# One DRAM read in place of five for the attention outputs of segments 0 to 2, with the features of a head dealt out in fives

## The chip, the core and the metric

The kernel runs on one core of a Trainium2 chip. The metric is device time in microseconds (us). The core has a matrix engine (PE), a vector engine (DVE), a scalar engine (ACT), a general one (POOL), and SyncE (SP), which here issues nearly all transfers. Each engine works through its own queue in the order in which it was written, and waits on semaphores for what other engines and transfers have to deliver. Matrix products go to PSUM, in eight banks; everything else is computed from SBUF.

## The reference

```python
# x: (2048, 640) bf16; H = 32 heads, Dh = 20; N = 4 segments of L = 512 tokens
q, k, v = heads of x @ wq, x @ wk, x @ wv
phi = lambda t: where(t > 0, t + 1, exp(t));  g = sigmoid(beta)
M = 0; z = 0                                     # a memory per head
for s in range(4):
    p = softmax(qs @ ks.T * Dh**-0.5 + causal mask)
    a_dot = p @ vs
    a_mem = (phi(qs) @ M) / (phi(qs) @ z + 1e-6)
    o[s] = g * a_mem + (1 - g) * a_dot
    M += phi(ks).T @ vs;  z += sum(phi(ks))
a = o @ wo
b = irfft2(rfft2(x) * (w_r + 1j * w_i))          # over tokens and features
t = sigmoid((x * gate_w).sum(-1))                # a gate per token
return t * a + (1 - t) * b
```

## The kernel before

There are two branches that share the engines: attention in four segments, and the two-dimensional spectral filter, done as matrix products with tables. Nothing decides an order at run time. The program lists its operations with their dependences, and a long tuple of numbers, `ORDER`, says in which order they go onto the five queues and, for operations that DVE or POOL could do, which of the two does it. A planner then places PSUM banks and semaphores along that order by rough costs (the `QUEUE` table has those of transfers); it moves nothing.

**Attention, segments 0 to 2.** Scores are computed for groups of four heads, exponentiated by ACT into `ex`, and masked by POOL (line 1299). The product with the values (`pv_flipped`) leaves outputs with features in rows, 32 rows a head (20 features, the denominator in row 20, padding), and 512 tokens in columns. ACT or DVE copies them to `ub`, and `st_u` stores two groups at a time in the DRAM scratch `u_scr` (3 segments of 1024 rows of 512 tokens). When a segment is done, `denominators` loads the denominators (`ld_den`, tile `dnc`), takes reciprocals (`dnr`), multiplies with the gate (`rc`) and stores the result in `r_scr` (`st_r`).

**The way back.** `finish_tile(s, 0)` loads the reciprocals (`ld_r`, tile `r`: each head's row in four partitions), and the outputs as `oU`: 128 partitions, four to a head, and five blocks `c` of 512 tokens, so that a partition has five of the head's 20 features. One load `ld_u` (line 1540) fills one block, for all 128 partitions. The `normal` step (line 1542, DVE or POOL) multiplies each block with `r`. For segments 1 and 2, `addmem` (line 1550) adds the memory's part: the memory was read in `mem_read`, divided by `mem_mul` (line 1172 for segments 1 and 2, 1175 for the last), stored in `o_scr`, and comes back by transposing loads as `mT`. The five blocks are then multiplied with the rows of `wo` that fit them (`ld_wo` loads these, one tile `wo` per block), in `finish_tile` (line 527 in the profile), which accumulates onto the gated spectral part and stores the result. Segment 3 goes another way, without `u_scr`.

**Where the blocks are written.** Each `oU` takes memory that something else used. For segment 0 it is that of the spectral branch's middle part (`after_mid`), for segment 1 the tile `phq`, for segment 2 the first values tile `va`.

**Around it.** While the way back runs, the spectral branch does its last part: 32 products of `Cp` with `big` into one PSUM bank each, which ACT or DVE copies to `eo`, or DVE combines with `eo` into `G` (line 1501). These and other single-bank products share four of the eight banks (`gen`); the scores have the other four. A gate per token goes through `omh`, `gT`, `g_scr`, `gbc` and `fbg`.

The way a block is dealt out before, in two lines of the code: row `4 * c + q` of a head goes to partition `q` of its four, block `c`; the same split stands in `ld_wo` and in `mem_mul`.

Of the kernel before, what the change touches and what calls it, by code (L numbers as in the profile page):

```python
# [12 lines left out]
P = 128  # L13
S = 2048
D = 640
H = 32
DH = 20
NSEG = 4
L = 512
KD = 321  # L20
VW = 22
# [424 lines left out]
def dap(ap, off, *dims):  # L446
    return bass.AP(tensor=ap.tensor, offset=ap.offset + off, ap=[list(q) for q in dims])
# [25 lines left out]
class Kern:  # L473
# [10 lines left out]
    def b(self, *key):  # L484
        v = self.bufs.get(key)
        if v is None:
            v = self.bufs[key] = Buf(str(key))
        return v
# [68 lines left out]
    def dma(self, dst, src, nbytes, r, w, prio, tr=False, name="", after=(), queue="sp"):  # L557
# [15 lines left out]
        "ld_hm": (600.0, 850.0, 16), "ld_r": (570.0, 700.0, 16), "ld_tt": (530.0, 1650.0, 16), "ld_u": (530.0, 600.0, 16),  # L573
# [86 lines left out]
        3616, 3446, 3618, 4034, 1577, 1610, 3156, 3176, 3620, 4016, 3622, 3158, 1634, 3154, 4102, 3606, 3624, 1636, 3626, 1638, 3178, 3628, 3448,  # L660
        3198, 3608, 3166, 1641, 1642, 3430, 3200, 1652, 3610, 3168, 1616, 1618, 3612, 4030, 1620, 1644, 3170, 1654, 1623, 1646, 4028, 3654, 1656,
        1648, 3160, 3184, 4042, 3584, 3656, 1658, 1650, 3162, 3670, 3250, 3658, 3587, 1688, 3146, 3660, 3672, 1690, 2940, 1692, 3164, 3187, 1624,
        1670, 1626, 4046, 1628, 4019, 1695, 3180, 2564, 1630, 3674, 1696, 1632, 1698, 3182, 1700, 3214, 3202, 1702, 1660, 3216, 1678, 3188, 1672,
        4036, 1680, 1674, 1662, 1704, 3462, 1664, 1682, 1676, 3588, 1666, 3206, 3218, 4038, 1742, 1684, 3204, 3208, 1750, 4020, 1744, 1668, 1746,
        3224, 1686, 3220, 1724, 1752, 1726, 4044, 1754, 1728, 1796, 3591, 3226, 1748, 3230, 3222, 1730, 3598, 1756, 3232, 3464, 1798, 3210, 1800,
        3600, 1732, 1758, 4080, 1734, 3228, 1736, 3602, 3238, 1803, 3470, 3212, 3604, 3630, 1738, 3240, 3706, 3234, 3632, 3638, 1740, 3708, 1706,
        3236, 3634, 1708, 3646, 3636, 1710, 4049, 4086, 3640, 3648, 3242, 1713, 3710, 4090, 3650, 3642, 1778, 4023, 3652, 1780, 3244, 3688, 3644,
        1714, 3690, 1716, 3246, 1782, 1804, 1718, 1806, 3692, 3694, 4024, 1808, 1720, 1760, 3714, 4082, 1784, 1810, 3662, 4089, 1722, 4094, 1850,
        3664, 1812, 3592, 1852, 1854, 3594, 1786, 3696, 3248, 1788, 1762, 1790, 4040, 1858, 1860, 4222, 1862, 4032, 1764, 1856, 4092, 3748, 1766,
        1792, 3678, 4206, 3750, 4208, 1864, 3666, 4210, 4098, 4212, 4214, 1794, 1768, 3676, 4510, 1770, 1866, 1772, 4216, 4026, 4050, 3596, 4064,  # L670
        4052, 4054, 4218, 3466, 3680, 1774, 3752, 1832, 4158, 3682, 1834, 3700, 1836, 1776, 4056, 4066, 3754, 4068, 3252, 4070, 4072, 4058, 4150,
        3668, 1840, 1842, 4074, 4154, 1838, 4084, 3756, 4076, 3698, 4146, 1844, 3758, 3716, 1814, 1846, 1816, 4142, 3702, 3718, 3720, 3684, 1848,
        4138, 3722, 3254, 3760, 4060, 4100, 3256, 4192, 4194, 3724, 3686, 4196, 3726, 4062, 3774, 4096, 1818, 4078, 3776, 1886, 3728, 3762, 4198,
        4200, 1820, 3468, 4202, 4104, 1888, 3778, 1822, 1824, 4224, 1826, 1890, 3766, 3786, 1828, 4354, 4226, 3764, 1893, 3768, 4228, 4230, 3780,
        1830, 4106, 4108, 4205, 4110, 3788, 4112, 4136, 4114, 4240, 3782, 4242, 4116, 4220, 4232, 3790, 4234, 4119, 3792, 3784, 3802, 3794, 3804,
        1894, 1896, 3704, 1898, 3806, 1900, 3808, 3770, 3796, 4244, 3772, 3810, 4236, 1902, 4246, 4248, 4250, 4238, 3812, 3798, 3852, 3814, 4120,
        3854, 4253, 3800, 4122, 4124, 1876, 4148, 4254, 3818, 3820, 4156, 1868, 3822, 4140, 4256, 1870, 1872, 4144, 3824, 1874, 4152, 3928, 3712,
        3826, 3732, 3828, 3930, 1878, 1880, 3734, 3736, 3830, 4160, 3856, 4320, 3738, 4357, 4176, 3932, 3740, 4126, 4178, 3742, 4128, 4130, 3744,
        4180, 4486, 3860, 4132, 4182, 3730, 3862, 1882, 3747, 4184, 4134, 4274, 4358, 4360, 4362, 3864, 4186, 4258, 4364, 4366, 4368, 4189, 3866,
        4418, 3920, 4370, 1884, 3858, 4490, 3922, 4276, 4322, 4260, 4372, 4262, 3868, 4374, 4452, 4376, 4378, 4380, 4264, 4278, 4382, 4280, 4492,  # L680
        4266, 3924, 4385, 3834, 4282, 3934, 3836, 4268, 4324, 4270, 4326, 3833, 4162, 4273, 4328, 4284, 4330, 4164, 4287, 4166, 3870, 4168, 4332,
        4170, 4288, 4334, 3816, 3842, 3838, 4336, 4402, 3844, 4404, 3872, 4406, 4172, 4408, 3936, 4388, 4175, 4338, 4340, 3874, 4390, 4342, 4190,
        4290, 3846, 4420, 4292, 4294, 4410, 3840, 4344, 4346, 4348, 3878, 3848, 4351, 4296, 3880, 4392, 4412, 4352, 3850, 4394, 4298, 4415, 3888,
        3876, 3890, 3892, 3894, 3882, 3884, 4304, 3896, 4396, 4300, 3898, 3886, 4398, 4306, 4302, 4308, 3938, 4454, 4400, 3904, 4488, 3940, 3906,
        4416, 3908, 3910, 3900, 3926, 4310, 4312, 3912, 4314, 4456, 3914, 4458, 4317, 4470, 4472, 3942, 3946, 3916, 4318, 4460, 3948, 4436, 3902,
        4474, 3944, 4462, 4464, 4438, 3950, 4466, 4440, 3952, 4442, 4469, 4476, 4444, 3958, 4478, 4422, 3964, 3954, 3974, 3960, 3966, 4480, 4424,
        4426, 3956, 4483, 4428, 4446, 4430, 4432, 4484, 3962, 3976, 3968, 3978, 4435, 4386, 3970, 3980, 4448, 4498, 3972, 3982, 4494, 3984, 3990,
        4450, 3992, 4496, 3986, 3994, 3996, 4500, 3989, 4548, 3998, 4526, 4512, 4000, 4620, 3919, 4514, 4002, 4528, 4634, 4516, 4622, 4004, 4636,
        4502, 4506, 4504, 4518, 4509, 4550, 4638, 4530, 4640, 4642, 4532, 4644, 4552, 4534, 4647, 4520, 4624, 4522, 4536, 4626, 4525, 4628, 4538,
        4562, 4564, 4566, 4568, 4546, 4540, 4630, 4570, 4554, 4633, 4542, 4544, 4598, 4556, 4600, 4572, 4654, 4648, 4602, 4604, 4575, 4558, 4650,  # L690
        4652, 4606, 4584, 4561, 4608, 4586, 4588, 4611, 4590, 4582, 4576, 4592, 4594, 4578, 4580, 4597, 4614, 4616, 4618, 4612,
# [183 lines left out]
    def late_weights(self):  # L875
        self.Sc.group += 1
        b = self.b
        for c in range(5):
            home = [b("pkn", t) for t in range(5)] if c < 4 else [b("phk", k, x * L) for k in range(2) for x in range(2)]
            self.dma(lambda c=c: self.wo[c].ap(0, [1, D]), lambda c=c: dap(self.wo_d, 4 * c * D, [DH * D, H], [D, 4], [1, D]),  # L880
                     P * D * 2, [], [b("wo", c)], self.texp(3, 0), name="ld_wo", after=home)
# [270 lines left out]
    def mem_read_tile(self, s, i, q, mine):  # L1152
# [18 lines left out]
        if s < 3:  # L1171
            fn = lambda e: e.tensor_tensor(self.mem.ap(i * D + 64 * q, [4, 16], [P, 5], [1, 4]), self.ps(bank, 0, [VW, 16], [4, 5], [1, 4]),
                                           dn.ap(16, [1, 16], [0, 5], [0, 4]), ALU.mult)
        else:
            fn = lambda e: e.tensor_tensor(self.mem.ap(i * D + q * 320, [DH, 16], [1, DH]), self.ps(bank, 0, [VW, 16], [1, DH]),  # L1175
                                           dn.ap(16, [1, 16], [0, DH]), ALU.mult)
# [345 lines left out]
    def finish_tile(self, s, a):  # L1522
# [8 lines left out]
        if s < 3:  # L1531
            oT = self.oU[s]
            ob = [b("oU", s, c) for c in range(5)]
            if a == 0:
                self.dma(lambda: self.r4[s].ap(0, [1, L]), lambda: dap(self.rd.ap(), s * H * L, [L, H], [0, 4], [1, L]), P * L * 2,
                         [b("rd", s)], [b("r4", s)], prio - 9.0, name="ld_r", after=[b("xT", 1, c) for c in range(5)])
                for c in range(5):
                    self.Sc.group += 1
                    home = self.after_mid(("oU", c)) if s == 0 else [b("phq", t) for t in range(5)] if s == 1 else [b("va", 0, lt) for lt in range(4)]
                    self.dma(lambda c=c: oT.ap(c * L, [1, L]), lambda c=c: dap(self.ud.ap(), (s * 1024 + 4 * c) * L, [32 * L, H], [L, 4], [1, L]),  # L1540
                             P * L * 2, [b("ud", s, i) for i in range(4)], [ob[c]], prio - 8.0, name="ld_u", after=home)
                    self.either(lambda e, c=c: e.tensor_tensor(oT.ap(c * L, [1, L]), oT.ap(c * L, [1, L]), self.r4[s].ap(0, [1, L]), ALU.mult),  # L1542
                                L, [b("r4", s)], [ob[c]], prio - 5.0, name="normal")
# [79 lines left out]
```

## Time and profile before

| | |
|---|---|
| Time, median of 3 runs | 242.59 us (242.13 to 242.78) |
| The profiled execution: its own time | 240.85 us |
| The profiled execution: its span | 238.9 us |
| Mean granted clock of PE | 0.998 |
| DMA, mean over the span | 177 GB/s |
| `oU<-u_scr` | 15 transfers of 128 KB, first issued at 164.8 us, last at 192.1 us |
| Multiply of line 1542 | 13 on DVE (362 to 868 ns), 2 on POOL (1156 ns) |
| Products of line 527 (segments 0 to 2) | from 185.9 us on |

The profile is of one execution. Its span runs from the first to the last recorded instruction; its own time is somewhat longer, and other executions differ again, so a sum that is made from the profile is made against 240.85 us and then moved by 1.74 us to stand beside the median. Engine rows say when an instruction started, how long it ran, the line that wrote it, and output and input tile; in square brackets, how long the engine stood idle before it and whose result it waited for. Rows of `SPq` are issues of transfers: they tell when the transfer was handed over, not when it landed. A neighbouring row of the same engine that overlaps by a few tenths of a microsecond is normal, since instructions are pipelined.

### The profile page before, as it was taken

To read this page: it belongs to the slowest core of one execution; us is meant where nothing else is said; L and a number is where in the kernel's file an instruction comes from. 1 tells how busy PE (TensorE), PEld (TensorE's weight loads), DVE (VectorE), ACT (ScalarE), POOL (GpSimd) and SP (SyncE) were. 2 spreads that over 40 slices of the span, in tenths; PEclk is the share of its full clock that TensorE was granted. 3 is DMA by queue.
4 is the path that set the end of the run, shared out by engine and by line. 5 is a ranking of instruction groups with operands and counts; after the bars stand their busy time and mean duration, and the time that the engine had idled before them with its cause. 6 is when DMAs were issued, how large, how long until landed. Compare 5 with 4: busy or idle time off the path is not lost.

```text
span 238.9 us, 10255 instructions
## 1 busy us (share of the span) xinstructions
PE 227.6 (95%) x4361; PEld 140.1 (59%) x4361; DVE 196.6 (82%) x481; ACT 199.5 (83%) x241; POOL 166.7 (70%) x297
## 2 busy tenths in 40 slices
PE   7899999999999999999989999999999999899994
PEld 2575566775456566555646655455645466567794
DVE  0579998889899996898999798997988896846563
ACT  2189688898899999999999979999899988797730
POOL 8523268457969956937974999875889868678730
PEclk9999999999999999999999999999999999999999
DMA  7999849996996876483779572364766995872223
GB/s 171 277 366 233 231 125 185 264 207 149 250 227 158 153 210 178 110 241 72 237 213 261 171 226 62 103 157 144 204 205 162 244 215 83 121 107 83 59 86 111
DMA packets 58928, 42.17 MB, mean 177 GB/s; under 512 B 30020, under 2 KB 55172, under 8 KB 58884
## 3 DMA queue, kind: packets, MB, share of 16 engines
q1 hardware_dynamic: 57844, 40.96, 69.9%
q8 instruction: 34, 0.56, 1.0%
q10 hardware_dynamic: 1040, 0.57, 0.8%
q14 instruction: 10, 0.08, 0.2%
HBM read 23.32 MB, written 12.30 MB: 149 GB/s over the span
## 4 chain that ended last, share of the span: by engine, by line
PE 54%; DVE 19%; ACT 14%; DMA 7%; issue 3%; SPq 1%; DVEq 0%
PE psum L529 48%; ACT ex L1278 9%; PE psum L527 6%; DVE Pt L1455 3%; DMA r_scr<-rc 3%; ACT et L1087 2%; DMA xT<-in_A_x_dram 2%; DMA Wt<-in_B_w_i_dram 2%; DVE xsb L921 2%; DVE xf L916 2%; DVE G L1501 1%; DVE va L1130 1%; DVE q L540 1%; DMA r<-r_scr 1%; DVE oU L1542 1%
## 5 line engine op out<-in xcount | busy, mean ns | idle before, releaser
L1278 ACT ACTIVATE ex<-psum 128x2048 bf16<-128x2048 f32 (+4 forms) x92 | 138.7, 1508 | 12.2 <-PE psum L529 10.1
L1299 POOL TENSOR_SCALAR_AFFINE_SELECT ex<-ex 128x256 bf16<-128x256 bf16 (+2 forms) x224 | 122.0, 567 | 37.2 <-ACT ex L1278 33.7
L529 PE MATMUL psum<-qkp 20*64 20x64 bf16 (+5 forms) x1280 | 32.3, 270 | 2.2 <-ACT ex L1278 2.0
L529 PE MATMUL psum<-xT,wk 128*128 128x256 bf16 (+1 forms) x280 | 33.9, 273 | 0.2
L529 PE MATMUL psum<-xT,wq 128*128 128x512 bf16 (+1 forms) x135 | 30.7, 380 | 0.8 <-DMA xT<-in_A_x_dram 0.8
L529 PE MATMUL psum<-wv,xT 128*32 128x321 bf16 (+3 forms) x400 | 30.0, 301 | 0.3 <-DVE va L1130 0.3
L1455 DVE TENSOR_TENSOR Pt<-psum,Wt 128x642 bf16<-128x642 f32 x32 | 25.6, 822 | 2.2 <-PE psum L529 1.9
L529 PEld LDWEIGHTS psum<-qkp 20*64 20x64 bf16 x1280 | 13.3, 102 | 19.7 <-ACT ex L1278 15.4
L529 PEld LDWEIGHTS psum<-xT,wk 128*128 128x128 bf16 (+1 forms) x280 | 19.9, 97 | 6.5 <-DMA wk<-in_A_wk_dram 0.6
L527 PE MATMUL psum<-wo,oU 128*32 128x320 bf16 x480 | 21.9, 300 | 0.7 <-DVE oU L1550 0.5
L921 POOL TENSOR_TENSOR xsb<-xf 128x320 bf16<-128x320 bf16 (+2 forms) x12 | 9.5, 790 | 16.1 <-DVE xsb L921 12.4
L529 PEld LDWEIGHTS psum<-wv,xT 128*32 128x32 bf16 (+1 forms) x400 | 14.6, 96 | 7.5 <-issue 2.6
L1130 DVE TENSOR_TENSOR va<-psum,ebx 128x320 bf16<-128x320 f32 x32 | 15.2, 484 | 4.4 <-ACT gate L1128 2.1
L529 PE MATMUL psum<-big,Ac 128*128 128x160 bf16 (+2 forms) x96 | 18.1, 258 | 0.4 <-DVE Pt L1455 0.3
L529 PE MATMUL psum<-big,Cp 128*128 128x321 bf16 (+1 forms) x96 | 18.0, 302 | 0.2 <-DVE G L1501 0.2
L529 PE MATMUL psum<-ex,va 128*32 128x64 bf16 (+3 forms) x576 | 17.4, 257 | 0.4 <-DVE mem L1175 0.2
L1501 DVE TENSOR_TENSOR G<-eo,psum 128x320 bf16<-128x320 f32 x32 | 14.7, 483 | 3.6 <-PE psum L529 2.6
L540 DVE CAST ot<-psum 128x320 bf16<-128x320 f32 x21 | 10.1, 491 | 9.1 <-PE psum L527 5.9
L529 PE MATMUL psum<-tt,Yt 128*128 128x256 bf16 (+1 forms) x96 | 16.5, 276 | 0.5 <-DVE Yt L1460 0.2
L529 PEld LDWEIGHTS psum<-ex,va 128*32 128x32 bf16 x576 | 10.8, 96 | 9.6 <-POOL ex L1299 1.3
L1087 ACT ACTIVATE et<-qu 128x512 bf16<-128x512 bf16 x25 | 15.6, 631 | 0.2
L527 PEld LDWEIGHTS psum<-wo,oU 128*32 128x32 bf16 x480 | 11.9, 96 | 5.4 <-issue 1.4
(99 smaller groups left out, 392.7 us busy)
## 6 DMA issues: line engine op xcount, KB each, us to landing
qkp<-qk_scr SPq DMA_DIRECT2D x28, 160.0 KB
tt<-tab_tt SPq DMA_DIRECT2D x8, 512.0 KB, 4.5
qk_scr<-qu SPq DMA_DIRECT2D x12, 256.0 KB, 3.1
u_scr<-ub SPq DMA_DIRECT2D x12, 256.0 KB, 3.7
xsb<-in_A_x_dram SPq DMA_DIRECT2D x8, 320.0 KB, 6.5
oU<-u_scr SPq DMA_DIRECT2D x15, 128.0 KB, 2.9
out_dram<-ot SPq DMA_DIRECT2D x12, 160.0 KB
Wt<-in_B_w_r_dram SPq DMA_DIRECT2D x16, 80.2 KB, 2.6
```

The lines of the kernel that those rows point to most:

```text
L527: h = e.matmul(dst, wt, r_, start=st, stop=sp_, **{**kw, "tile_position": (0, q), "skip_group_check": True})
L529: h = e.matmul(o_, l_, r_, start=st, stop=sp_, **kw)
L540: alts["dve"] = (lambda e: e.tensor_copy(dst(), src()), 67 + 1.04 * n, 68.0)
L916: self.either(lambda e, r=r, op=op: e.tensor_tensor(xf.ap(r * 642, [321, 2], [1, 320]), xs.ap(o, [D, 2], [1, 320]), xs.ap(o + 320, [D, 2], ...
L921: self.either(lambda e, dst=dst, src=src, d0=d0, n=n, op=op: e.tensor_tensor(xs.ap(o + dst, [D, 2], [1, n]), xf.ap(src + d0, [321, 2], [1, ...
L1087: self.one("act", lambda e: e.activation(et.ap(0, [1, L]), qsl(), ACT.Exp), L, [qb], [b("et", pi_)], late, fix=95, name="phi_exp")
L1130: self.one("dve", lambda e: e.tensor_tensor(va.ap(i * H * VW + h0 * VW, [VW, nh], [1, DH]), self.ps(bank, 0, [DH, nh], [1, DH]), self.ebx. ...
L1278: self.one("act", lambda e, d=d, q=q: e.activation(self.ex.ap(*d), self.ps(bank, *q), ACT.Exp, scale=SC), n, [bank], [self.exb(s, 2 * pr + ...
L1299: self.one("pool", lambda e: e.affine_select(self.ex.ap(e0 + d0, [1280, 4], [1, n], np_=np_), self.ex.ap(e0 + s0, [1280, 4], [1, n], np_=np_),
L1455: self.one("dve", lambda e, ri=ri, Pt=Pt, Wt=Wt, wo_=wo_, bank=bank: e.tensor_tensor(Pt.ap(ri * 322, [644, 2], [1, KD]), self.ps(bank, 0, ...
L1501: self.one("dve", lambda e, q=q, n2=n2, bank=bank, eo=eo: e.tensor_tensor(self.G.ap(n2 * D + 639 * q, [1 - 2 * q, 320]), eo.ap(q, [1, 320] ...
L1542: self.either(lambda e, c=c: e.tensor_tensor(oT.ap(c * L, [1, L]), oT.ap(c * L, [1, L]), self.r4[s].ap(0, [1, L]), ALU.mult), L, [b("r4", ...
```

## The change

Each segment's five `ld_u` become one transfer that fills all five blocks. For that, the features of a head are dealt out the other way: row `5 * q + c` goes to partition `q`, block `c`, so that a partition's five rows follow one another in `u_scr`, 5120 B in one run. `ld_wo` and `mem_mul` follow with the same split. The multiplies stay five for a segment. In `ORDER` the numbers of the four loads that are gone are missing, and the later ones are renumbered; the one load stands at the place of the segment's last. The instruction order of PE, DVE, ACT and POOL is that of before. In the planner's table the load's cost is set anew.

```diff
-        ... "ld_u": (530.0, 600.0, 16),
+        ... "ld_u": (640.0, 3000.0, 16),
...
# late_weights
-    lambda c=c: dap(self.wo_d, 4 * c * D, [DH * D, H], [D, 4], [1, D])
+    lambda c=c: dap(self.wo_d, c * D, [DH * D, H], [5 * D, 4], [1, D])
...
# mem_read_tile, s < 3
-    fn = lambda e: e.tensor_tensor(self.mem.ap(i * D + 64 * q, [4, 16], [P, 5], [1, 4]), self.ps(bank, 0, [VW, 16], [4, 5], [1, 4]),
+    fn = lambda e: e.tensor_tensor(self.mem.ap(i * D + 64 * q, [4, 16], [P, 5], [1, 4]), self.ps(bank, 0, [VW, 16], [1, 5], [5, 4]),
                                    dn.ap(16, [1, 16], [0, 5], [0, 4]), ALU.mult)
...
# finish_tile, s < 3, a == 0, after ld_r
+    home = []
+    for c in range(5):
+        home += self.after_mid(("oU", c)) if s == 0 else []
+    home = home if s == 0 else [b("phq", t) for t in range(5)] if s == 1 else [b("va", 0, lt) for lt in range(4)]
+    self.Sc.group += 1
+    self.dma(lambda: oT.ap(0, [1, 5 * L]),
+             lambda: dap(self.ud.ap(), s * 1024 * L, [32 * L, H], [5 * L, 4], [1, 5 * L]),
+             P * 5 * L * 2, [b("ud", s, i) for i in range(4)], ob[:5], prio - 8.0, name="ld_u", after=home)
     for c in range(5):
         self.Sc.group += 1
-        home = self.after_mid(("oU", c)) if s == 0 else [b("phq", t) for t in range(5)] if s == 1 else [b("va", 0, lt) for lt in range(4)]
-        self.dma(lambda c=c: oT.ap(c * L, [1, L]), lambda c=c: dap(self.ud.ap(), (s * 1024 + 4 * c) * L, [32 * L, H], [L, 4], [1, L]),
-                 P * L * 2, [b("ud", s, i) for i in range(4)], [ob[c]], prio - 8.0, name="ld_u", after=home)
         self.either(lambda e, c=c: e.tensor_tensor(oT.ap(c * L, [1, L]), oT.ap(c * L, [1, L]), self.r4[s].ap(0, [1, L]), ALU.mult),
                     L, [b("r4", s)], [ob[c]], prio - 5.0, name="normal")
```

## The prediction, made before the changed kernel ran

> **What bounds the kernel now.** I read the page first: the busy shares and the 40 slices.
>
> ```profile
> PE 227.6 (95%) x4361; PEld 140.1 (59%) x4361; DVE 196.6 (82%) x481; ACT 199.5 (83%) x241; POOL 166.7 (70%) x297
> ...
> PE   7899999999999999999989999999999999899994
> ```
>
> TensorE (PE) is busy nearly everywhere, so time is lost where PE is made to wait and won only where it waits already. The change touches the stretch from 164 to 205 us, so I read the timeline there, engine by engine. First SyncE's DMA queue (start, length, both in us):
>
> ```profile
> 172.51 1.13 SPq L563 DMA_DIRECT2D u_scr<-ub  x1
> 173.68 0.48 SPq L563 DMA_DIRECT2D qk_scr<-qu  x1
> 174.19 0.53 SPq L563 DMA_DIRECT2D oU<-u_scr  x1
> ...
> 181.68 0.39 SPq L563 DMA_DIRECT2D u_scr<-ub  x1
> ...
> 184.12 0.51 SPq L563 DMA_DIRECT2D dnc<-u_scr  x1
> 184.68 1.29 SPq L561 DMA_TRANSPOSE mT<-o_scr  x1
> 186.02 0.59 SPq L563 DMA_DIRECT2D oU<-u_scr  x1
> ...
> 189.52 3.17 SPq L563 DMA_DIRECT2D oU<-u_scr  x5
> 192.74 0.60 SPq L563 DMA_DIRECT2D r_scr<-rc  x1
> ```
>
> 174.19 is the fifth and last load of segment 0's outputs; the first was issued at 164.85. 186.02 is the last of segment 1 (first at 179.77), and 189.52 holds all five of segment 2. Next who uses them, on VectorE (DVE), then GpSimd (POOL):
>
> ```profile
> 172.69 0.42 DVE L1542 TENSOR_TENSOR oU<-oU,r 128x512 bf16<-128x512 bf16 x1
> ...
> 184.25 1.56 DVE L1542 TENSOR_TENSOR oU<-oU,r 128x512 bf16<-128x512 bf16 x3
> 185.73 1.67 DVE L1501 TENSOR_TENSOR G<-eo,psum 128x320 bf16<-128x320 f32 x4
> ```
>
> ```profile
> 183.19 1.16 POOL L1542 TENSOR_TENSOR oU<-oU,r 128x512 bf16<-128x512 bf16 x1
> ```
>
> The multiply at 172.69 is segment 0's first, and runs before the fifth load is even issued. Of the three at 184.25 the first two are segment 0's last, the third (from 185.3) is segment 1's; POOL's at 183.19 is segment 1's as well. Both run before 186.02. Last, PE right behind the first place, and the DMA view for transfer times (KB each, us from issue to landing):
>
> ```profile
> 174.95 1.00 PE L529 MATMUL psum<-big,Cp 128*128 128x321 bf16 x6 [0.17 <-DVE G L1501]
> ```
>
> ```profile
> tt<-tab_tt SPq DMA_DIRECT2D x8, 512.0 KB, 4.5
> ...
> oU<-u_scr SPq DMA_DIRECT2D x15, 128.0 KB, 2.9
> ```
>
> At 174.95 PE waits for a sum that DVE (G, line 1501) reads out of a PSUM bank: there DVE has no lead over PE.
>
> **The change, part by part.** Instruction order on PE, DVE, ACT and POOL is the same in both builds. On SP, twelve `ld_u` issues go, and each segment's one transfer stands where the last of its five stood: behind `qk_scr<-qu` (173.68), behind the transpose of 184.68, and at 189.52. It writes all five parts of `oU`, so the first multiply of a segment now waits for all 640 KB.
>
> *How long 640 KB take.* Low bound: the 128 KB load at 174.19 landed in 2.5 us; the DMA engines moved 294 GB/s at a share of 0.92 in 174 to 176, so 320 GB/s full, and 512 KB more take 1.6: 4.1 us. High bound for a quiet queue: from 128 KB in 2.5 to 512 KB in 4.5 is 2.0 us per 384 KB, so 2.7 more: 5.2 us. I take 4.6 us, nearer to the low end since the runs in DRAM grow from 1 KB to 5 KB. [...]
>
> *Segment 0.* SP can't come earlier by much: `u_scr<-ub` at 172.51 waits for ACT's copy of `ub` (171.89 to 172.48), which does not move. The transfer starts between 173.5 (if that issue takes its median 0.46 us instead of 1.13) and 174.2; I take 174.0, landing 178.6. DVE stands at 172.69 until then: 5.9 us. Behind it in DVE's queue are the G sums of 173.02 and 173.60; PE needs their banks by 174.95 with no slack, so it stops as long. POOL's small gate product at 175.41 needs DVE's cast of 173.42, and stops too, inside the same gap. Some comes back: DVE then no longer waits 0.78 us for ACT's `eo` at 176.47, nor PE 0.21 for ACT at 176.16, since ACT catches up in the gap. I take 0.5 back (bounds 0 and 0.9). **Net +5.4 us.**
>
> *Segment 1,* told in the clock of the old trace; all of it lies later by the above. SP reaches the transfer no earlier though two loads at 182.62 are gone: `dnc` before it waits for `u_scr<-ub`, issued 181.68 and landed 2.4 us later, at 184.1. So issue stays 186.02. The load there took 4.3 us for 128 KB, with two others just ahead that now are gone. Bounds 4.1 and 4.3+2.7=7.0; I take 5.2, nearer the quiet case: landing 191.2. DVE stands from 185.3: 5.9 us. PE has some lead here: it has projections of segment 0 (185.9 on), whose inputs are done and whose banks ACT empties; it needs the next G bank at 187.2, and the first sum of 185.73 is done after two pieces at 186.55, so 0.6 us of lead. **Net +5.3 us** (bounds 3.6 and 7.7). POOL waits longer, 183.19 to 191.2, and then has the masks of 184.29 (2.57 us) to do, ready near 195. PE takes the first scores of segment 3 that need them at 190.93, shifted 196.2: covered by a little over a microsecond. If that cover goes, POOL's delay of 8 us leads, some 2 us more.
>
> *Segment 2.* The one transfer issued at 189.5 lands by about 195; its multiplies ran at 201.75, held by `r` alone (0.6 us). That `r` hung on `r_scr<-rc`, 6.70 us in the chain, queued behind five `oU` loads; now the queue is drained when `rc`, later by DVE's delay, is stored. `r` then arrives ahead of DVE, which saves that 0.6 us and PE's wait of 0.47 at 205.63. **Net -0.6 us** (bounds -1.2 and 0).
>
> *The rest.* SP is freed of 12 issues of 0.6 us, 7.1 us; nothing on the path waits for SP there. `mem_mul` (16 at 0.488 us) now reads PSUM with a step of 5 inside: I cost it at nothing, since DVE's `ub` copy, with a step of 16, takes 0.686 us and the unstrided `qu` copy 0.681; the bounds are 0 and 16 times 0.005, and a gain is excluded as no element less is read. `ld_wo` still moves 1280 B rows, 160 KB in 3.2 us, long before use: nothing, and what hides it is the time from 117.7 and later to the first projection at 185.9.
>
> **Sum:** 5.4+5.3-0.6 = +10.1 us on the profiled execution's own 240.85 us (span 238.9): 251.0. The median shown is 1.74 above that execution, so 252.7 us.
>
> **Rivals.**
> 1. *POOL or a slow transfer leads* at segment 1: the queue there already gave 4.3 us for 128 KB. With 7.0 us DVE's stand is 7.7 and POOL's 9.8; total +12 to +14.5, 254.6 to 257.1. Against: the two loads that made that queue are gone. 0.17.
> 2. *Half hidden:* transfers at 4.1 us, more given back by PE: 4.0+3.6-1.2 = +6.4, 249.0; a little below if the lead of PE at 187.2 is larger. For: engines idle in the stall and catch up; PE has 3.6 us of gaps after 206. Against: those gaps are waits inside short chains of the same engines. 0.13.
> 3. *The other side, faster:* fewer, larger transfers empty the queue, and the chain through `r_scr<-rc` (6.70) and `r` (2.26) shortens. It gains the 0.6 and 0.5 us above, 241.5, if neither stand exists. It decides only where the 640 KB land by 172.7 and 185.3, so are issued by 168.1 and 180.1. Against: SP's places 174.19 and 186.02, fixed by `ub` and `dnc`. [...] 0.03.
> 4. *No change:* the work behind DVE's waits is not needed in time, or the loads did not move. Against: the 0.17 at 174.95, and the build. 0.02.
>
> The forecast itself gets 0.65. The range, 248.5 to 256.5, holds the forecast with its bounds, rival 2, and most of rival 1. Slower by over 0.3% (about what a measurement here can tell from no change): 0.95; within 0.02; faster 0.03.
>
> **What would show it.** In the changed profile: one `oU<-u_scr` of 640 KB at 173.5 to 174.2, landing in 4 to 5 us; a wait of DVE's `oU` multiply for it of about 6 us from 172.7, then another of about 6, and one of POOL near 8; PE's slices near 175 and near 192 of the span falling to about half; segment 2's multiply waiting for no DMA, and `r_scr<-rc` landing in about 3 us. I am wrong if those waits are under 2 us, if PE keeps busy through them, or if a third wait shows.

## The result, and the profile after

| | before | after |
|---|---|---|
| Median, runs on the same chip | 242.69 us (241.60 to 246.01, 6 runs) | 258.05 us (256.90 to 259.88, 6 runs) |
| Ratio, 95% interval | | 1.0661 (1.0615 to 1.0707) |
| The profiled execution: own time, span | 240.85 us, 238.9 us | 257.58 us, 255.6 us |
| Mean granted clock of PE there | 0.998 | 0.966 |

Medians and ranges take in every execution; ratios leave out those that took over 1.5% longer than the fastest of their kernel, so a ratio need not be the quotient of the medians. The change costs 15.4 us; the forecast was 10.1 us, and 258.05 us lies above its range. The page of after, PE's busy time, its 40 slices (6.4 us each) and the clock granted to it:

```profile
PE 232.9 (91%) x4361; PEld 141.3 (55%) x4361; DVE 198.0 (77%) x481; ACT 199.9 (78%) x241; POOL 166.5 (65%) x297
...
PE   7799999999999999998999999994697399999994
...
PEclk9999999999999999999999999998589779999999
```

PE executes as many matmuls as before and is busy 5.3 us longer with them. The slices fall in two places (to 4 and 6 tenths from 172 us, to 7 and 3 from 192 us), and the clock falls at both. Before, the clock row had a 9 in every slice. The SyncE queue in the timeline of after (start, length):

```profile
175.17 0.52 SPq L563 DMA_DIRECT2D oU<-u_scr  x1
...
192.85 0.53 SPq L563 DMA_DIRECT2D dnc<-u_scr  x1
193.43 1.29 SPq L561 DMA_TRANSPOSE mT<-o_scr  x1
194.76 0.58 SPq L563 DMA_DIRECT2D oU<-u_scr  x1
...
198.94 0.59 SPq L563 DMA_DIRECT2D oU<-u_scr  x1
```

One transfer a segment, in the foretold places. The multiplies wait for them (line 1542 is 1547 in the changed file), as the timelines of VectorE and then GpSimd show (in brackets the idle time ahead, and who ended it):

```profile
179.75 0.42 DVE L1547 TENSOR_TENSOR oU<-oU,r 128x512 bf16<-128x512 bf16 x1 [5.70 <-DMA oU<-u_scr]
...
200.28 0.43 DVE L1547 TENSOR_TENSOR oU<-oU,r 128x512 bf16<-128x512 bf16 x1 [6.35 <-DMA oU<-u_scr]
...
218.41 2.09 DVE L1547 TENSOR_TENSOR oU<-oU,r 128x512 bf16<-128x512 bf16 x5 [0.46 <-DMA r<-r_scr]
```

```profile
200.33 1.39 POOL L1547 TENSOR_TENSOR oU<-oU,r 128x512 bf16<-128x512 bf16 x1 [8.17 <-DMA oU<-u_scr]
```

The third multiply waits for no outputs. PE in the same stretches:

```profile
175.34 0.31 PE L529 MATMUL psum<-big,Cp 128*128 128x321 bf16 x1
180.63 0.99 PE L529 MATMUL psum<-big,Cp 128*128 128x321 bf16 x3 [4.98 <-DVE G L1501]
182.15 1.79 PE L529 MATMUL psum<-big,Cp 128*128 128x321 bf16 x6 [0.53 <-ACT eo L538]
...
197.13 0.32 PE L529 MATMUL psum<-G,fbg 128*32 128x320 bf16 x4 [0.80 <-ACT ot L538]
201.95 0.46 PE L529 MATMUL psum<-G,fbg 128*32 128x320 bf16 x4 [4.50 <-DVE G L1501]
...
204.37 1.79 PE L527 MATMUL psum<-wo,oU 128*32 128x320 bf16 x24
```

A stand is a stretch in which PE has no work it may start; the waits of 4.98 and 4.50 us are the two large ones. The third row and the last are what the prediction did not have: those six matmuls took 1.00 us before (the row at 174.95), and the 24 of the last row 1.00 us (at 188.85). Windows of 2 us tell why (busy time and instructions of PE, PEld, DVE, ACT, POOL, then the granted clock, DMA share, GB/s):

```profile
176.00:178.00 2.00, 0.00 (x0) 0.00 (x0) 0.00 (x0) 1.38 (x1) 0.71 (x2) 0.69 0.97 236
...
184.00:186.00 2.00, 2.00 (x24) 0.98 (x21) 1.00 (x4) 1.55 (x2) 0.00 (x0) 0.50 0.12 27
186.00:188.00 2.00, 2.00 (x47) 0.99 (x46) 1.25 (x5) 1.07 (x2) 1.39 (x3) 0.75 0.67 184
...
200.00:202.00 2.00, 0.05 (x4) 0.05 (x8) 1.72 (x5) 0.00 (x0) 1.67 (x2) 0.67 1.42 278
202.00:204.00 2.00, 2.00 (x27) 0.73 (x27) 1.97 (x5) 0.37 (x1) 1.93 (x4) 0.50 1.04 278
```

At both stands the clock was halved while PE stood and stayed halved when PE was full again: from 178 to 180 us it was 0.50 with no matmul, and at 184 to 186 us PE was busy for the whole 2 us at a clock of 0.50. Adding up the shortfall of such windows (a window of 2 us at 0.69 holds 2 x 2 x 0.31 = 1.2 us of half clock; the windows left out read 0.50 from 178 to 184 us and at 204, and 0.63 at 206 us), the clock was halved for 10.2 us at the first stand and 6.8 us at the second.

How the 16.7 us between the two profiled executions are made up, by the start of the same PE work in both: 1.3 us were there before 172 us; from there to the products of `ex` and `va` behind the first stand (188.96 us after, 180.06 before) 7.6 more; across the second stand, up to the products of `wo` at 213.60 us (196.83 before), 7.9 more; and nothing that matters from there to the end. Over the first of these stretches PE was busy 11.04 us instead of 8.46, over the second 18.92 instead of 16.44: 2.6 and 2.5 us longer for the same matmuls.

### The profile page after: what moved, and what is told of

Its sections match the earlier page's. It is cut to its first block, busy times and chain, and to the rows that moved or that the text cites. A ratio compares the mean times of both kernels' runs of the same rounds, so it can differ in the third digit from the quotient of the medians.

```text
span 255.6 us, 10244 instructions
## 1 busy us (share of the span) xinstructions
PE 232.9 (91%) x4361; PEld 141.3 (55%) x4361; DVE 198.0 (77%) x481; ACT 199.9 (78%) x241; POOL 166.5 (65%) x297
## 4 chain that ended last, share of the span: by engine, by line
PE 48%; ACT 15%; DMA 15%; DVE 14%; SPq 4%; issue 2%
PE psum L529 43%; ACT ex L1278 11%; PE psum L527 6%; DMA oU<-u_scr 4%; DVE Pt L1455 3%; SPq L561 3%; DMA qkp<-qk_scr 2%; DMA wk<-in_A_wk_dram 2%; DMA r<-r_scr 2%; DMA pkn<-phk 2%; ACT et L1087 2%; DMA tt<-tab_tt 2%; SPq L563 2%; DVE G L1501 1%; DVE oU L1547 1%
## 5 line engine op out<-in xcount | busy, mean ns | idle before, releaser
L529 PE MATMUL psum<-qkp 20*64 20x64 bf16 (+5 forms) x1280 | 32.9, 274 | 2.0 <-ACT ex L1278 1.3
L529 PE MATMUL psum<-big,Cp 128*128 128x321 bf16 (+1 forms) x96 | 20.6, 335 | 5.5 <-DVE G L1501 5.0
L527 PE MATMUL psum<-wo,oU 128*32 128x320 bf16 x480 | 23.1, 313 | 0.5 <-DVE oU L1555 0.5
L1501 DVE TENSOR_TENSOR G<-eo,psum 128x320 bf16<-128x320 f32 x32 | 14.7, 482 | 3.7 <-PE psum L529 3.5
L1547 DVE TENSOR_TENSOR oU<-oU,r 128x512 bf16<-128x512 bf16 x13 | 7.8, 627 | 12.5 <-DMA oU<-u_scr 12.0
L529 PE MATMUL psum<-tt,Yt 128*128 128x256 bf16 (+1 forms) x96 | 16.5, 276 | 0.4 <-DVE Yt L1460 0.2
L529 PEld LDWEIGHTS psum<-ex,va 128*32 128x32 bf16 x576 | 10.9, 97 | 10.1 <-POOL ex L1299 1.4
```

The source lines that it names most:

```text
L527: h = e.matmul(dst, wt, r_, start=st, stop=sp_, **{**kw, "tile_position": (0, q), "skip_group_check": True})
L529: h = e.matmul(o_, l_, r_, start=st, stop=sp_, **kw)
L1501: self.one("dve", lambda e, q=q, n2=n2, bank=bank, eo=eo: e.tensor_tensor(self.G.ap(n2 * D + 639 * q, [1 - 2 * q, 320]), eo.ap(q, [1, 320] ...
```

## The experiments

**Which part costs it.** The expectations tell these theories apart: the time goes to the stands behind the late place of each segment's transfer, slow clock included ("A" where they use letters); it goes to the new layout ("C"); the engines work off a backlog behind the stands, at full clock ("B"); it goes to the 640 KB transfer as such, wherever it is issued ("D"); or to PSUM banks that the planner places differently because the load's entry in its cost table changed ("E"). Each kernel is timed beside runs of before, whose medians were 242.49 us (experiments 1 to 4), 243.62 us (7 to 10) and 242.27 us (5, 6, 11 and 12); across these groups the ratios are compared. As to the banks, the programs of experiments 1, 5, 6, 7 and 12 use those of before throughout; those of 2, 4, 8 and 10 share one other set; 11 has the set of the change; 3 and 9 have each their own.

**1. The layout alone**: features in fives, but five loads in the places of before.

```diff
+    MERGED = ()      # segments with one transfer; the others load each block:
+    self.dma(... oT.ap(c * L, [1, L]), dap(self.ud.ap(), (s * 1024 + c) * L, [32 * L, H], [5 * L, 4], [1, L]), ..., name="ld_u")
```

> Only the way the features are dealt out is new (loads of wo, the PSUM read of mem_mul, the rows of the five loads); each segment still has five loads, at their old places. Theory A (the loss is two stands of VectorE's queue, each followed by a stretch of TensorE at half clock): 242.6 us, within 0.5. Rival C (the new dealing-out costs part of the 15.4 us, in the strided PSUM read or the loads of wo): 244 to 247 us. If C holds, mem_mul is slower than 0.488 us.

Measured 242.41 us, ratio 0.9997 (0.9961 to 1.0033). The step of 5 in `mem_mul` (median 0.488 us each in the profile of after, 0.488 before) and the other split of `wo` cost nothing that can be measured. One of its executions, the profiled one, took 246.84 us; it comes back in the last section.

**2 and 3. One segment alone**: one transfer in the place of the change, for segment 0 or for segment 1; the other segments with five loads as in experiment 1.

```diff
-    MERGED = ()
+    MERGED = (0,)    # or (1,)
```

> Features in fives as in the change, but only segment 0 comes back in one transfer, at the place of its old fifth load; segments 1 and 2 keep five loads at their places. Theory A: a DVE wait of about 5.7 us and PE at half clock for some microseconds behind it, +7.6 us over before, 250.2. The recorded sum, without a clock term: +5.4, 248.0. Rival B (engines work off a backlog after the stand, at full clock): also about +7.6, but with the granted clock at 1.0 throughout.

> The same with segment 1 alone in one transfer, at the place of its old fifth load. Theory A: a DVE wait of about 6 us, a POOL wait of about 8 us, PE at half clock behind it, +7.9 us, 250.5. The recorded sum: +5.3, 247.9. If the two stands only cost what they did because they stood in one run, e2 and e3 together fall well short of +15.4.

Segment 0: 249.61 us, ratio 1.0314 (1.0272 to 1.0357), +7.1 us; VectorE waited 5.48 us and PE 4.76 + 0.53 us, and the clock was halved for 10.2 us as in the change. Segment 1: 248.00 us, ratio 1.0250 (1.0199 to 1.0302), +5.5 us, less than was expected. PE's row of it, and its windows:

```profile
193.63 0.32 PE L529 MATMUL psum<-G,fbg 128*32 128x320 bf16 x4 [3.66 <-DVE G L1501]
```

```profile
192.00:194.00 2.00, 0.37 (x12) 0.23 (x12) 2.00 (x6) 0.00 (x0) 2.00 (x3) 1.00 1.21 325
194.00:196.00 2.00, 2.00 (x31) 0.66 (x27) 1.97 (x4) 1.04 (x1) 1.93 (x4) 0.51 1.08 258
196.00:198.00 2.00, 2.00 (x30) 0.80 (x22) 2.00 (x2) 1.17 (x2) 2.00 (x5) 0.64 0.38 121
```

Here PE stood 0.84 us less than in the change (3.66 against 4.50), and the clock, still 1.00 when PE started again, was halved for 3.4 us where the change had 6.8. The two together give +12.6 of the +15.4 us; these two differences, 0.84 us and up to half of 3.4 us, come to 2.5 and would account for nearly all of what is left. That is not shown: two of the four executions had a lower mean clock (0.985 against 0.991) and took 247.79 and 248.95 us, no clearly longer than the others (248.21 and 247.76 us), and the banks differ too. Why the half-clock stretch was shorter was not tested.

**4. All three merged, at the places of each segment's first load.**

```diff
-    MERGED = (0,)
+    MERGED = (0, 1, 2)   # ORDER: the transfer where ld_u of the segment's first block stood
```

> All three segments in one transfer each, as in the change, but at the place of each segment's first old load instead of its last. Theory A: no DVE wait over 1 us (POOL may wait 1 to 2 us at segment 1, where the first place is 179.8), clock at 1.0, time 241.5 to 243.0 us. Rival D (a 640 KB transfer is itself the harm, since smaller ones queue behind it): 245 us or more wherever it stands.

Measured 247.46 us, ratio 1.0142 (1.0054 to 1.0230): missed, the expectation was no loss. The four executions spread from 244.16 us (mean clock 0.998) to 248.57 us (0.986). In the profiled one, the longest, no multiply of VectorE waited for outputs. Instead, in the timeline of PE:

```profile
178.24 1.77 PE L529 MATMUL psum<-big,Cp 128*128 128x321 bf16 x6 [1.71 <-ACT eo L538]
```

The wait is now for a bank that ScalarE empties (`eo`), where the row of before had 0.17 us for VectorE's `G`; the clock fell here too (0.57 from 178 to 182 us), as 1.77 us for six matmuls shows. Either the larger transfer did it, or the banks.

**5. The same with the banks of before**: the load's entry in the planner's cost table set back, nothing else.

```diff
-    "ld_ua": (640.0, 3000.0, 16)    # the one transfer of a segment
+    "ld_ua": (530.0, 600.0, 16)
```

> One transfer for each segment at the place of the first old load, as before, but with the planner's cost for it left at the old load's, so that PSUM banks fall as in the kernel before. Theory E (what the early places lost, 3.4 us, came from other banks: TensorE waited 1.7 us for ScalarE's copy of eo, and its clock fell): no such wait, 241 to 243 us. Rival D (the large transfer itself): 244 us or more, with the loss after 180 us behind the transfers.

Measured 242.50 us (12 runs), ratio 1.0032 (1.0003 to 1.0060). The same transfers in the same places, and the wait is back to what it was:

```profile
177.79 1.00 PE L529 MATMUL psum<-big,Cp 128*128 128x321 bf16 x6 [0.17 <-DVE G L1501]
```

The two programs differ in banks alone, so the wait for `eo`, and the half clock behind it, came from the banks. By the ratios they cost 2.7 us there, but the intervals of experiments 4 and 5 just meet. The 640 KB transfer as such costs 0.6% at most, and it gains nothing.

**6. How much of the change is banks**: the change's own places, with an entry that gives the banks of before.

```diff
-    "ld_ua": (640.0, 3000.0, 16)
+    "ld_ua": (0.0, -5000.0, 16)
```

> The changed kernel, late places and all, with a planner's cost for the transfer chosen so that PSUM banks and TensorE's waits fall as in the kernel before. If the two stands and the clock are all of it: 257 to 258.5 us, as the change. Theory E for the change too (part of the loss is other banks): 0.5 to 2 us faster, 256 to 257.5.

Measured 256.66 us, ratio 1.0626 (1.0586 to 1.0667), against 1.0661 (1.0615 to 1.0707) for the change: the banks are 0.8 us of the loss by the ratios, and since the intervals overlap, perhaps nothing. With the banks of before the late places alone cost 6%. Its waits are those of the change (VectorE 11.6 us in two, GpSimd 8.2 us, PE 4.74 and 5.65 us).

**7. Segment 2 alone, merged at the late place** (`MERGED = (2,)`).

> Segment 2 alone in one transfer, where its five stood together. Theory A: nothing waits for it; the recorded sum has -0.6 us, the profile of the change about -0.1. So 242.0 to 242.7 us. If it costs over 1 us, a third term was overlooked.

Measured 242.18 us, ratio 0.9965 (0.9885 to 1.0044). No wait for outputs, and no gain that can be told from none.

**8. Segment 0 at a place in between**: `MERGED = (0,)`, the transfer issued at 171.44 us instead of 174.62 (experiment 2).

> Segment 0 alone in one transfer, but three places on SyncE's queue earlier than in the change: right behind the store of the reciprocals of segment 1, ahead of the store of ub that waits for ScalarE. It is then issued near 171 us and lands near 175.5: a DVE wait of 2 to 3 us in place of 5.7. Theory A (the clock falls only when TensorE goes without matmuls for some four microseconds): PE's gap is about 2 us, the clock stays at 1.0, +1.5 to +2.5 us, 244.1 to 245.1. Rival B (a surcharge in proportion to the stand, 7.6 for 5.7): +3 to +4 us, 245.6 to 246.6. If the clock falls after so short a gap too: +4 us or more.

Measured 245.00 us, ratio 1.0069 (1.0001 to 1.0137), +1.4 us. In the profiled execution (249.72 us, the longest of the four) VectorE waited 1.24 us for the outputs instead of 5.48, and PE's waits shrank with it (0.52 us for `G`, 1.01 us for `eo`); for `r` of segment 2 it waited 2.0 us. The clock was to stay at 1.0 and did not: it was halved for 3.4 us from 179.8 us, and later for 6.8 us from 210.2 us, around a stop of the kind told in the last section (worked out from PE's rows, 1.55 us for five products of `Cp` at 179.62 us against 0.85 in experiment 9, and 1.78 us for 24 of `wo` at 215.43 us against 1.00; the mean clock of 0.979 over 247.8 us makes 10.4 us in all). The four microseconds of theory A are near PE's longest waits in experiments 2 and 3 (4.76 and 3.66 us); as a threshold no run shows them, and here the clock fell behind shorter waits. Experiments 2, 4 and 8 have the same programs on the four engines, banks included, so between 2 and 8 the loss goes with the place; what is left may be the banks' wait for `eo`, as in experiment 4.

**9. Late places, but nothing queued behind the wait.** The change's transfers, with the multiplies moved back on VectorE and GpSimd to where the data has landed: segment 0's first two to before the third, segment 1's on GpSimd behind a later mask, its two on VectorE behind later work.

```diff
# ORDER, VectorE, around segment 0 (names in place of numbers, cut)
-    G  G  G  normal(0)  G  omh  G ... normal(0)  normal(0) ...
+    G  G  G             G  omh  G ... normal(0)  normal(0)  normal(0) ...
```

> All three segments in one transfer at the late places of the change, but five multiplies are moved back in VectorE's and GpSimd's order: two of segment 0 to stand beside its other two, behind the memory read, two of segment 1 behind the gate product of segment 2, and GpSimd's of segment 1 behind the next nine masks. Theory A (what costs is the waiting multiply ahead of the sums that TensorE needs, not the late transfer): no DVE wait over 1 us, clock at 1.0, 242 to 244 us. If TensorE itself needed the blocks earlier, the stands move to its projections and the time stays above 248.

Measured 244.03 us, ratio 1.0049 (0.9998 to 1.0100). PE's row at the first place reads as before the change:

```profile
175.80 1.00 PE L529 MATMUL psum<-big,Cp 128*128 128x321 bf16 x6 [0.17 <-DVE G L1501]
```

No multiply waited for outputs, though the transfers were as late (174.56 us for segment 0). What costs nearly all of the 15.4 us is the queue behind the waiting multiply, not the lateness. The clock was to stay at 1.0 throughout; it was halved once, for 3.4 us from 197.8 us, in a wait of PE of 0.99 us for segment 1's blocks (`addmem`): 16 products of `wo` took 1.28 us at 199.24 us and 0.72 at 186.74, and the mean clock was 0.993 in all four executions (3.4 us of half clock over 242.0). That may be the 0.5% left.

**10. Is the clock a cost of its own?** Experiment 2 with 16 extra matmuls, which nobody reads, in the stand, into a scores bank that is free then. They fill PE without shortening VectorE's wait.

```diff
         bank = Bank(4, "qk")
+        if (s, pr, u) == (2, 3, 4):
+            self.mms([(lambda: (self.ps(bank, 0, [1, 384]), self.fcat.ap(0, [1, P]), self.fcat.ap(0, [1, 384]), True, True, {}), 384)
+                      for _ in range(16)], [b("fcat"), bank], [], prio - self.QK_LEAD, name="fill", mode=0)
```

> As the run with segment 0 alone in one late transfer, with 16 extra matmuls of 128x384 put into TensorE's queue where it stands; their result is never read. They wait for ScalarE to empty the score banks, near 177.4 us, and would run 2.6 us at full clock, inside the stand. Theory A: TensorE's gap is cut to under 2 us, the clock stays up, and the same DVE wait of 5.7 us costs 5 to 6 us instead of 7.6: about 2 us faster than the run without them. Rival B (backlog of other engines): no faster, since the fill helps no other engine; if the clock has fallen before they start, they run 5 us and the time is slower than without them.

PE's timeline and a window:

```profile
177.39 2.77 PE L529 MATMUL psum<-fcat 128*128 128x384 bf16 x16 [1.79 <-ACT ex L1281]
180.13 0.59 PE L529 MATMUL psum<-big,Cp 128*128 128x321 bf16 x3
181.25 1.00 PE L529 MATMUL psum<-big,Cp 128*128 128x321 bf16 x6 [0.53 <-ACT eo L538]
```

```profile
180.00:182.00 2.00, 1.47 (x11) 0.71 (x9) 2.00 (x7) 0.44 (x1) 1.76 (x5) 1.00 0.00 0
```

VectorE waited as before (5.24 us against 5.48), but the clock stayed at 1.00 and the six matmuls took 1.00 us. From the twelve score products ahead of the stand to the second group of twelve behind it, PE took 16.5 us, against 19.5 in experiment 2 and 11.7 in before: the stand costs 4.8 us with the clock kept and 7.8 without. The whole time missed its expectation all the same: 252.06 us, ratio 1.0337 (1.0251 to 1.0423), no better than experiment 2. In its profile the 3 us are lost again later, at two stops of PE for which the trace names nobody, and the clock was halved for 3.4 us behind the second:

```profile
208.83 0.34 PE L529 MATMUL psum<-va,ex 128*128 128x21 bf16 x7 [1.02 <-issue]
...
215.85 0.29 PE L529 MATMUL psum<-qkp 20*64 20x64 bf16 x16 [2.39 <-issue]
```

**11. The change itself with such fills**, 16 in the first stand and 22 in the second.

```diff
-        if (s, pr, u) == (2, 3, 4):
+        if (s, pr, u) in {(2, 3, 4): 16, (3, 0, 2): 22}:
```

> The changed kernel with unread extra matmuls of 128x384 in TensorE's queue inside both stands: 16 at the first, 22 at the second. Theory A (half clock behind each stand): clock at 1.0 behind both stands; in the profile the first stand costs about 4.8 us instead of 7.6 and the second about 5.5 instead of 7.9, so the sum comes down from +15.4 to about +10, the recorded sum without a clock term; 252 to 254 us unless the stops of unknown cause seen near 205 to 216 us in other runs add to it. Rival B (backlog): stays at 257 us or more, with the same cost of each stand.

Measured 254.08 us, ratio 1.0539 (1.0493 to 1.0585): 4.0 us less than the change by the medians, 3.0 by the ratios, the intervals apart, although 38 matmuls were added. VectorE still waited 5.15 and 5.56 us (1.3 us less than in the change, over both) and GpSimd 7.37 us.

```profile
194.55 3.75 PE L529 MATMUL psum<-fcat 128*128 128x384 bf16 x22
...
199.72 1.00 PE L527 MATMUL psum<-wo,oU 128*32 128x320 bf16 x24
```

The 24 products of `wo` behind the second stand took 1.00 us here and 1.79 us in the change (at 204.37 us), and the clock was 1.00 from 170 to 204 us; there it fell after all, for 3.4 us. In two of the other executions the mean clock was 1.000, and they took 253.59 and 254.15 us. So part of the loss was the clock: 3 to 4 us over the whole time, of which up to 1.3 us may be the shorter waits.

**12. Is there a version that gains?** Segment 0 merged at its first place, segment 2 merged late, segment 1 with five loads, banks as before (`MERGED = (0, 2)`).

> Candidate for the best: segment 0 in one transfer at its first place, segment 2 in one at its place, segment 1 in five as before (its first place is too late for one: GpSimd waited 0.9 us there), old banks. 241.0 to 242.5 us: no wait for oU on VectorE or GpSimd; a gain over before of at most 1 us.

Measured 243.11 us (12 runs), ratio 1.0034 (0.9992 to 1.0075). No gain, so none of the versions run here beats the kernel before.

## Why the prediction was right in direction and wrong in size

*Places and transfers: right.* Segment 0's transfer was foretold at 174.0 us and stands at 175.17, of which 1.3 us is the later start of that execution; segment 1's at 186.02 in the old clock, and is there (194.76 less 1.3 and 7.6 is 185.9). From issue to the multiply that it released took 4.6 us (forecast 4.6) and 5.5 us (forecast 5.2). That longer runs in DRAM bring a transfer nearer to the low bound was the author's estimate; no experiment changes their length alone.

*The waits: right.* VectorE 5.70 and 6.35 us (5.9 and 5.9), GpSimd 8.17 us (near 8), no third one. Of PE, 4.98 + 0.53 us at the first stand and 0.80 + 4.50 us at the second make 10.8 us idle; the two terms of the sum were 5.4 + 5.3 = 10.7.

*The step that failed* is how those two terms were closed: "so it stops as long" was taken for the whole price of a stand, with PE at full speed from its first matmul on. The work behind a stand was so put at no extra cost, without a reason. The stands cost 7.6 and 7.9 us, 2.1 and 2.6 more than the waits of PE in them. That is what a halved clock adds to PE's work behind a stand: PE's busy time grew by 2.6 and 2.5 us, and experiments 10 and 11 took most of it away with nearly the same waits of VectorE (3.1 us at one stand; 3 to 4 us over both, the shorter waits included). The clock row of before had 9 everywhere, so nothing in that trace showed the price; but PE had no stop of this length in the stretch that I read, and a stop of a new length should have been a rival with a bound. The trace of after shows what the two stands (4.98 and 4.50 us as PE's longest waits) cost here, 2.1 to 2.6 us beyond all the waits in them; the last section has falls of the clock at shorter gaps.

*The bounds of the layout: right.* Experiment 1 has 0.9997. The banks were not in the prediction at all: that the instruction order is the same does not mean that the banks are. By the ratios they are worth 0.8 us in the change and 2.7 us at the early places (experiments 4 and 5), both with intervals that meet.

*Segment 2:* forecast -0.6 us; in the change the 16.7 us less 1.3, 7.6 and 7.9 leave -0.1, and experiment 7 is too wide to tell. `r` was to arrive ahead of VectorE; VectorE waited 0.46 us for it instead of 0.61. With the `oU` loads gone from ahead of `r_scr<-rc`, `r` was issued at 213.20 us, 4.0 us behind that store, and the multiply started 5.2 us later; before, the load took 2.26 us. In the new queue a transposing load stands right ahead of it and a store of results right behind.

*The rivals.* GpSimd as the leader (0.17) had a time near the measured one, 254.6 to 257.1 us, by another mechanism: behind its 8.17 us PE did not wait for a mask. Only with the clock kept (experiment 11) does a mask show, with 0.67 us. Half hidden (0.13) is out: PE's idle time grew by 5.1 and 5.4 us, so at most the half microsecond that the sum had was given back, and the transfers took 4.6 and 5.5 us instead of 4.1. That larger transfers help (0.03) is refuted for its own condition: with the stands gone, experiments 5 and 12 found no gain.

## What to carry to other kernels

Here the first multiply behind a merged load waited for the whole of it (5.70 and 6.35 us on VectorE, where five loads had cost no wait), and all that was queued behind it waited too. Move the load to the place of the first part, or the consumer behind other work, before merging; here each cost 1% at most (experiments 5 and 9). Price a new stop of a busy TensorE like these as the wait plus the work behind it at half clock (here 2.1 to 2.6 us on stops of 5.3 to 5.5), and after any edit of costs or sizes compare the PSUM banks too, not only the instruction order.

## What the runs showed of the hardware

*How long the clock stayed halved.* From the windows, 10.2 and 6.8 us in the change, 10.2 us in experiment 2, and 3.4 us each in experiments 3, 10 and 11. In experiment 6 it was 14.7 us in all, worked out from the mean clock of 0.971 over a span of 253.8 us. In the change the two falls, worked out from the windows of 0.69 and 0.67, lie at 176.8 and 200.7 us, 1.1 and 3.2 us after PE's last matmul ended. In these runs the length of a gap alone does not decide: PE's gap of 1.71 us in experiment 4 was followed by a fall, and that of 1.79 us in experiment 10 was not; experiment 9 has a fall in a gap of 0.99 us. What else counts, and what sets these lengths, was not tried.

*Stops without a visible cause.* In some executions PE stops for 1 to 2.4 us near 203 to 216 us, with "issue" as the only releaser: the two in experiment 10, 1.59 us in experiment 4 (at 204.58 us), 2.13 us in the longer execution of experiment 1 (at 210.35 us), whose other executions took from 241.67 us on. A stop of 1.50 us is in experiment 8 (at 214.39 us), one of 0.20 us in before. The times of experiment 1 suggest that they come in some executions of a kernel and not in others; their cause is open.
